# A state exchange layer on one core: one small-matmul stretch per batch, at the change of batch, in place of two

## The chip, the cores and the metric

The kernel runs on 1 core of one Trainium2 chip. The metric is the device time of one execution in microseconds (us). Before the change it was 646.53 us, the median of 3 runs (646.25 to 646.66).

## What is computed

The reference has two parts. The first, for each of 8 batches and 8 heads, exchanges 512 tokens `x` (512 x 64) with 32 states (32 x 64) by two softmaxes; the second sends the 4,352 rows that come out (8 batches x (512 tokens + 32 states), 512 wide) through two weight matrices.

```python
a  = softmax(x @ state.T / 8)        # over the 32 states
xread = a @ state                    # 512 x 64: what the tokens read
a2 = softmax(state @ x.T / 8)        # over the 512 tokens
sread = a2 @ x                       # 32 x 64: what the states read
x  = rows of [xread; sread], heads side by side   # 4352 x 512
h  = x @ w_in                        # 512 -> 2048
g  = where(h >= 1, h, where(h <= -1, 0, (h + 1)**2 / 4))
out = g @ w_out                      # 2048 -> 512
```

## The kernel before

**Order of the work.** The hidden width of 2048 is cut into 8 chunks of 256 (`NJ = 8`, index `j`). For a batch `b` and a chunk `j` the kernel makes `h` (`g1`, L488: two products of 6 matmuls each, L448 to L450), bends it to `g` on ACT and DVE (`relu`, `square`, `bound`, `high`, `low`), and adds `g` times a chunk of `w_out` to four accumulators of 128 tokens (`g2`, L502: 24 matmuls, L524 to L526). `g2` of a chunk is issued one step late, behind `g1` of the next chunk, so TensorE has work while ACT and DVE bend. Values are split into a high and a low part (`h` and `l` in the names), and each product is three matmuls: high x high, low x high, high x low. All of these big matmuls have a 128x128 tile of weights and 512 moving columns. A step of one chunk is 12 + 24 = 36 of them.

**No xread.** The kernel never forms `xread`. It multiplies the states of a batch with `w_in` first (`sw_product`, L371; tiles `sw_c`, named by the first chunk c that they hold), so that `h = a @ (state @ w_in)`. Such a product of one chunk is 16 small matmuls (L383, 64x32 of weights, 256 columns, 8 places of the array in turn). Two chunks together fill a pair of PSUM banks. ACT then copies the high part out (`sw_high`, L404, ACT instruction L623), and DVE subtracts to get the low part (`sw_low`, L408, L410); only then are the banks free. Eight chunks make four such pairs: chunks 1 and 2, 3 and 4, 5 and 6, and 7 with chunk 0 of the next batch.

**The attention of the next batch** runs beside this: `scores` (L217, 16 matmuls of 512 columns, tile `sc`), both softmaxes on DVE and ACT, and `shuffle`, 16 DMAs on SP's queue that turn the second softmax's weights (tile `e2`; `e` in the profile). `read2` (L326, L334: 64 small matmuls, 128x32 of weights and 64 columns, tile `sr`) forms `sread` from `e2` and the loaded `x` (tile `xn`, `load_xn`, L187). `scale2` (DVE, tile `rs`) divides by the sums. `keep2` (L346) turns the result with a TensorE transpose (tile `rt`, L348) and `keep` (L352) has ACT copy it into `srT`, which after the last batch goes through the two weight matrices as a last, ninth batch.

**PSUM.** There are eight banks: four accumulators (`ps_acc`, tag `acc`), two for `h` (`ps_h`), and one double tile (`ps_mm`) that scores, `sr` and `rt` share.

**What sets the order.** Batch 0 is emitted from an order written out by hand (`SEQ`), which the change does not touch. Batches 1 to 7 follow the program's loop (L875 on); within it, `later(place, b, j, ...)` hangs the attention's steps on a place of a step (`mid`: after `g1`; `end`: after `g2`). In a step with `j == 0` stands a stretch of small matmuls: the pairs 1, 3, the next scores, the pair 5. In the step with `j == 5`, between the two halves of `g2`, stands a second one: `read2` of the next batch and the pair 7. In batch 1 `read2` of its own states stands by itself behind `g1` of chunk 0. Each engine takes its instructions in order and waits with semaphores for others; SP's queue issues the DMAs in order.

Of the kernel before, what the change touches and what calls it, by code (L numbers as in the profile page):

```python
# [8 lines left out]
F32 = mybir.dt.float32  # L9
F32R = mybir.dt.float32r  # L10
# [94 lines left out]
def state_exchange_moe(  # L105
# [17 lines left out]
    nc = tc.nc  # L123
    B, P, NT, H, D = x.shape
    S = NT * P
    NS = 32
    DM = H * D
    NPR = H // 2
# [9 lines left out]
    small = ctx.enter_context(tc.tile_pool(name="small", bufs=1))  # L138
    const = ctx.enter_context(tc.tile_pool(name="const", bufs=1))
    work = ctx.enter_context(tc.tile_pool(name="work", bufs=2))  # L140
    ps = ctx.enter_context(tc.tile_pool(name="ps", bufs=2, space=PSUM))
    wop = ctx.enter_context(tc.tile_pool(name="wop", bufs=NJ))
    rawp = ctx.enter_context(tc.tile_pool(name="rawp", bufs=2))

    def ps_acc(name):
        return ps.tile([P, DM], F32, tag="acc", bufs=4, name=name)
# [4 lines left out]
    def ps_mm(name):  # L151
        return ps.tile([P, 2, 512], F32, tag="mm", bufs=1, name=name)
# [19 lines left out]
    srT = const.tile([P, NPR, B, NS], F32, name="srT")  # L172
# [5 lines left out]
    loaded = {}  # L178
# [8 lines left out]
    def load_xn(b):  # L187
        xn = work.tile([P, NT, H, D], F32, tag="xn", bufs=1, name=f"xn{b}")
        nc.sync.dma_start(out=xn, in_=x[b])
        return xn  # L190

    class Attention:
# [146 lines left out]
        def scale2(self):  # L339
# [3 lines left out]
                out=self.rs, in0=self.sr[:, :, :D], in1=self.r2[:, :, None].broadcast_to([P, 2, D]), op=ALU.mult  # L343
            )

        def keep2(self):  # L346
            self.rt = ps_mm(f"rt{self.b}")
            nc.tensor.transpose(  # L348
                out=self.rt[:, 0, :P], in_=self.rs.rearrange("p a d -> p (a d)"), identity=ident
            )  # L350
# [5 lines left out]

    def split_tiles(name, spare=False):
        if spare:  # L360
            both = rawp.tile([P, 2, 1024], F32R, tag="raw", name=f"{name}hl")
            return both[:, 0], both[:, 1]
        hi = work.tile([P, 1024], F32R, tag="wh", name=f"{name}h")
        lo = work.tile([P, 1024], F32R, tag="wl", name=f"{name}l")
        return hi, lo
# [2 lines left out]

    sw_of = {}

    def sw_product(items, apart=None, spare=False):  # L371

        b, c = items[0]
        if apart:
            banks = [apart(f"sw{b}_{c}_{hh}") for hh in range(2)]
        else:
            pt = ps_mm(f"sw{b}_{c}")
            banks = [pt[:, hh] for hh in range(2)]
        for i, (bi, ci) in enumerate(items):
            for pr in range(NPR):  # L380
                for hh in range(2):
                    rows = slice(hh * 64, hh * 64 + 64)
                    nc.tensor.matmul(  # L383
                        banks[hh][pr * NS:(pr + 1) * NS, i * CI:(i + 1) * CI],
                        lhsT=sb[rows, bi, pr], rhs=w32[ci][rows, pr], start=True, stop=True,
                    )
        w = len(items) * CI
        if b == 0 and c < NH:
            whole = work.tile([P, 1024], F32, tag="wh", name=f"sw{b}_{c}w").rearrange("p (q f) -> p q f", q=2)[:, :, :w]
            sw_of[b, c] = [(banks[q][:, :w], whole[:, q], None) for q in range(2)]  # L390
            chunk[b, c] = whole, None
            return
        wh, wl = (
            v[:, :2 * w].rearrange("p (q f) -> p q f", q=2) for v in split_tiles(f"sw{b}_{c}", spare)
        )
        if apart:
            sw_of[b, c] = [(banks[q][:, :w], wh[:, q], wl[:, q]) for q in range(2)]
        else:
            sw_of[b, c] = [(pt[:, :, :w], wh, wl)]
        for i, item in enumerate(items):  # L400
            cols = slice(i * CI, (i + 1) * CI)
            chunk[item] = wh[:, :, cols], wl[:, :, cols]

    def sw_high(b, c, engine="ACT"):  # L404
        for pt, wh, _ in sw_of[b, c]:
            copy(engine, wh, pt)

    def sw_low(b, c):  # L408
        for pt, wh, wl in sw_of[b, c]:
            nc.vector.tensor_tensor(out=wl, in0=pt, in1=wh.bitcast(F32), op=ALU.subtract)  # L410
# [91 lines left out]
    def g2(b, j, half=None):  # L502
        n = n_of[b]
        per = S // n
        nt = n // P
        if b not in acc:
            acc[b] = [ps_acc(f"acc{b}_{t}") for t in range(nt)]
        gh, gl = gs[b, j]
        last = j == NJ // per - 1
        pairs = [(i, t) for i in range(2 * per) for t in range(nt)]  # L510
        if last:
            pairs.sort(key=lambda p: p[1])
        if half is not None:
            pairs = pairs[half * len(pairs) // 2:][:len(pairs) // 2]
        for i, t in pairs:
            f = 2 * per * j + i
            oh, ol = wo[f // 2][:, 0, f % 2], wo[f // 2][:, 1, f % 2]
            c0 = (i % per) * n + t * P
            lh, ll = (v if v is None else v[:, i // per, c0:c0 + P] for v in (gh, gl))
            a = acc[b][t]  # L520
            if ll is None:
                nc.tensor.matmul(a, lhsT=lh, rhs=ol, start=f == 0, stop=False)
                continue
            nc.tensor.matmul(a, lhsT=lh, rhs=oh, start=f == 0, stop=False)  # L524
            nc.tensor.matmul(a, lhsT=lh, rhs=ol, start=False, stop=False)  # L525
            nc.tensor.matmul(a, lhsT=ll, rhs=oh, start=False, stop=f == NF - 1)  # L526
            if last and i == 2 * per - 1:
                store(b, t)
# [90 lines left out]
    def copy(engine, out, src):  # L619
        if engine == "DVE":  # L620
            nc.vector.tensor_copy(out, src)
        else:
            nc.scalar.copy(out=out, in_=src)  # L623
# [28 lines left out]
    atts = {}  # L652
# [153 lines left out]
    for word in GROUPS.split():  # L806
        c, n = word.split(".")
# [16 lines left out]
    def later(place, b, j, *items):  # L824
        for f, *a in items:
            background.setdefault((place, b, j), []).append((f, a))

    def issue(place, b, j):

        for f, a in background.get((place, b, j), ()):  # L830
            f(*a)

    def attention(b):

        def at(place, j, *names):
            for name in names:
                f, *q = name.split()
                later(place, b - 1, j, (lambda f=f, q=q: getattr(atts[b], f)(*map(int, q)),))

        at("end", 1, "turn 0", "turn 1", "top2 0")  # L840
        at("mid", 2, "exp2 0", "top2 1", "exp2 1", "top1 0", "top1 1", "turn_blocks 0")
        at("mid", 3, "turn_blocks 1", "shuffle")
        at("end", 3, "less1 0", "less1 1")
        at("end", 4, "exp1 0", "exp1 1", "sum1 0", "sum1 1", "inv1")
        at("mid", 5, "norm1 0", "norm1 1", "back 0", "back 1")
        at("mid", 6, "high1 0", "rest 0", "high1 1", "rest 1")
        at("end", 6, "keep2", "keep")

    def states_split():
        sh, sl = (work.tile([P, NPR, B * NS], F32R, tag=t, name=f"s{t}") for t in ("ath", "atl"))  # L850
# [2 lines left out]
        nc.vector.tensor_tensor(out=sl, in0=src, in1=sh.bitcast(F32), op=ALU.subtract)  # L853
        att_of[B] = (sh, sl)

    def load_later(b):
        loaded["xn", b] = load_xn(b)

    for name in ("read2", "scale2"):
        later("mid", 1, 0, (lambda name=name: getattr(atts[1], name)(),))  # L860
    later("mid", 1, 1, (load_later, 2))
    for name in ("keep2", "keep"):
        later("mid", 1, 3, (lambda name=name: getattr(atts[1], name)(),))
    for b in range(2, B):
        attention(b)
    for c in range(NG):
# [8 lines left out]
    with guard:  # L875
        plan.emit(warm, "sc.0.1", "g2.0.0.0")
        for i, (b, j) in enumerate(steps):
            if j == 0 and 1 < b < B - 1:
                load_later(b + 1)
            prior = steps[i - 1] if i else (0, NJ - 1)  # L880
            hid = g1(b, j, split=j or b == B)
            issue("mid", b, j)
            if j == 0 and b < B:
                g2(*prior, 0)
                hid.high()
                hid.low()
                g2(*prior, 1)
                sw_product([(b, 1), (b, 2)], ps_h)
                sw_product([(b, 3), (b, 4)], ps_acc)
                if b + 1 < B:  # L890
                    att_start(b + 1)
                sw_product([(b, 5), (b, 6)], ps_acc, True)
                for c in (1, 3, 5):
                    sw_high(b, c)
                    sw_low(b, c)
            elif j == 5 and b < B:
                g2(*prior, 0)
                if b + 1 < B:
                    atts[b + 1].read2()
                sw_product([(b, 7), (b + 1, 0)][:B - b], ps_h)  # L900
                sw_high(b, 7)
                sw_low(b, 7)
                if b + 1 < B:
                    atts[b + 1].scale2()
                g2(*prior, 1)
            else:
                g2(*prior)
            if j == 1 and b + 2 < B:
                loaded["xt", b + 2] = load_xt(b + 2)
            issue("end", b, j)  # L910
        g2(*steps[-1])


# [41 lines left out]
```

## Time and profile before

| | us |
|---|---|
| median of 3 runs | 646.53 |
| profiled execution | 646.69 |
| its span, first to last instruction | 644.9 |
| TensorE matmuls (PE) busy | 636.8 |
| TensorE weight loads (PEld) busy | 512.2 |
| ACT busy | 370.8 |
| DVE busy | 355.1 |
| mean granted TensorE clock | 1.000 |

Times are from the start of the span. PE is TensorE's matmuls, PEld its weight loads, which run beside them; DVE, ACT and SP are the vector, scalar and synchronization engines. L383 is line 383 of the kernel. A row of the timeline has the start, the length, the engine, the line, the operation, `out<-in`, the shapes and how many instructions in a row were merged; what the engine waited for stands in brackets behind. Matmuls are pipelined, so that the rows of a stream overlap: a big matmul shows 0.39 us, and the next starts 0.23 us later. What counts for TensorE is therefore the distance from start to start, not the busy time. A batch takes 71.6 us (its stretches in chunk 0 start at 99.77 and 171.53 us).

### The profile page before, as it was taken

Reading aid. Unit: us, or ns where it says so; the run is one execution under the profiler, and the core shown is the slowest. Engines: PE = TensorE matmul, PEld = TensorE weight load, DVE = VectorE, ACT = ScalarE, POOL = GpSimd, SP = SyncE. Lnnn points to the kernel's source line nnn. Section 1 sums busy time; section 2 is a strip of 40 time slices with the busy share of each in tenths; the row PEclk is TensorE's granted clock in tenths of the full one; section 3 lists DMA queues with packets and bytes.
Section 4 is the critical chain, followed back from the end, with each engine's and each line's share of the span. In section 5 each row is a group of like instructions: output and inputs, shape, how many; then the busy total and the mean of one; then the engine's idle time right before and its main releaser. Section 6 shows DMA issues by size and latency. Waiting matters only on the chain.

```text
span 644.9 us, 10366 instructions
## 1 busy us (share of the span) xinstructions
PE 636.8 (99%) x4358; PEld 512.2 (79%) x4358; DVE 355.1 (55%) x515; ACT 370.8 (57%) x542; POOL 0.8 (0%) x7
## 2 busy tenths in 40 slices
PE   8999999999999999999999999999999999999997
PEld 6667787878788787878788787878788778878896
DVE  5999965554465535664465535553465535335431
ACT  4999755555555555555755455545755455454641
POOL 0000000000000000000000000000000000000000
PEclk9999999999999999999999999999999999999999
DMA  8996115021201203030302212030102010000101
GB/s 354 415 373 233 41 21 197 0 52 48 106 26 28 71 16 116 6 93 2 131 1 33 67 41 90 14 87 1 66 1 33 1 67 2 1 0 1 66 1 33
DMA packets 41550, 47.33 MB, mean 73 GB/s; under 512 B 31776, under 2 KB 31904, under 8 KB 38432
## 3 DMA queue, kind: packets, MB, share of 16 engines
q1 hardware_dynamic: 41168, 46.35, 20.9%
q8 instruction: 34, 0.56, 0.4%
q10 hardware_dynamic: 336, 0.33, 0.2%
q14 instruction: 12, 0.10, 0.0%
HBM read 34.08 MB, written 8.91 MB: 67 GB/s over the span
## 4 chain that ended last, share of the span: by engine, by line
PE 94%; ACT 3%; DMA 1%; DVE 1%; issue 0%
PE acc L524 19%; PE acc L525 19%; PE acc L526 19%; PE h L448 10%; PE h L449 10%; PE h L450 10%; PE sw L383 4%; PE sc L217 1%; PE sr L334 1%; PE warmed L165 1%; DMA sb<-in_state_dram 1%; ACT u L465 1%; ACT raw_o L578 0%; ACT raw_i L578 0%; ACT raw_o L570 0%
## 5 line engine op out<-in xcount | busy, mean ns | idle before, releaser
L524 PE MATMUL acc<-wo,gh 128*128 128x512 f32 x544 | 213.2, 392 | 0.0
L525 PE MATMUL acc<-wo,gh 128*128 128x512 f32 x544 | 211.9, 390 | 0.1
L526 PE MATMUL acc<-wo,gl 128*128 128x512 f32 x544 | 211.8, 389 | 0.0
L472 DVE SCALAR_TENSOR_TENSOR u<-u,h 128x512 f32<-128x512 f32 x136 | 92.8, 687 | 180.2 <-ACT u L469 179.5
L465 ACT ACTIVATE u<-h,half 128x512 f32<-128x512 f32 x136 | 93.1, 690 | 159.0 <-PE h L450 156.7
L486 DVE TENSOR_TENSOR gl<-u,gh 128x1024 fp32r<-128x1024 f32 x68 | 83.3, 1225 | 75.8 <-ACT gh L623 75.7
L524 PEld LDWEIGHTS acc<-wo,gh 128*128 128x128 f32 x544 | 102.1, 188 | 26.3 <-issue 3.7
L526 PEld LDWEIGHTS acc<-wo,gl 128*128 128x128 f32 x544 | 102.1, 188 | 21.3
L525 PEld LDWEIGHTS acc<-wo,gh 128*128 128x128 f32 x544 | 102.2, 188 | 21.0 <-DVE wo L608 0.4
L623 ACT CAST gh<-u 128x1024 fp32r<-128x1024 f32 x68 | 71.5, 1052 | 40.8 <-DVE u L472 40.7
L469 ACT ACTIVATE u<-u 128x512 f32<-128x512 f32 (+1 forms) x128 | 84.5, 660 | 4.0
L383 PE MATMUL sw<-w,sb 64*32 64x256 f32 x1024 | 33.5, 380 | 0.0
L539 ACT COPY o<-acc 128x512 f32<-128x512 f32 x33 | 19.1, 586 | 16.6 <-PE acc L526 16.6
L383 PEld LDWEIGHTS sw<-w,sb 64*32 64x32 f32 x1024 | 17.9, 106 | 13.0 <-issue 7.6
L449 PE MATMUL h<-ath,sw_3l 128*128 128x512 f32 x64 | 25.0, 391 | 0.2 <-DVE sw_3l L410 0.2
L448 PE MATMUL h<-ath,sw_3h 128*128 128x512 f32 x64 | 25.0, 391 | 0.0
L450 PE MATMUL h<-atl,sw_3h 128*128 128x512 f32 x64 | 24.9, 390 | 0.0
L448 PE MATMUL h<-ath,sw_1h 128*128 128x512 f32 x60 | 24.3, 405 | 0.6 <-DVE u L472 0.6
L448 PE MATMUL h<-ath,sw_7h 128*128 128x512 f32 x60 | 23.9, 399 | 0.0
L450 PE MATMUL h<-atl,sw_1h 128*128 128x512 f32 x60 | 23.4, 390 | 0.0
L450 PE MATMUL h<-atl,sw_7h 128*128 128x512 f32 x60 | 23.4, 390 | 0.0
L449 PE MATMUL h<-ath,sw_1l 128*128 128x512 f32 x60 | 23.4, 390 | 0.0
(166 smaller groups left out, 711.9 us busy)
## 6 DMA issues: line engine op xcount, KB each, us to landing
xt<-in_xt_dram SPq DMA_DIRECT2D x16, 512.0 KB, 4.8
raw_i<-in_moe_w_in_dram SPq DMA_DIRECT2D x8, 1024.0 KB, 7.2
raw_o<-in_moe_w_out_dram SPq DMA_DIRECT2D x8, 1024.0 KB, 9.3
xn<-in_x_dram SPq DMA_DIRECT2D x8, 1024.0 KB, 5.6
out_dram<-o SPq DMA_DIRECT2D x32, 256.0 KB, 2.0
e<-eb SPq DMA_DIRECT2D x112, 32.0 KB, 2.0
sb<-in_state_dram SPq DMA_DIRECT2D x1, 448.0 KB, 11.6
out_dram<-o SPq DMA_DIRECT2D x4, 64.0 KB, 1.7
```

Source lines behind the costliest of these rows:

```text
L383: nc.tensor.matmul(banks[hh][pr * NS:(pr + 1) * NS, i * CI:(i + 1) * CI], lhsT=sb[rows, bi, pr], rhs=w32[ci][rows, pr], start=True, stop=True,
L448: nc.tensor.matmul(o, lhsT=wh[:, k, sl], rhs=ah[:, k], start=first, stop=False)
L449: nc.tensor.matmul(o, lhsT=wl[:, k, sl], rhs=ah[:, k], start=False, stop=False)
L450: nc.tensor.matmul(o, lhsT=wh[:, k, sl], rhs=al[:, k], start=False, stop=last)
L465: nc.scalar.activation(out=self.u[:, i], in_=self.hs[i], func=AF.Relu, scale=0.5, bias=half)
L469: nc.scalar.activation(out=u, in_=u, func=AF.Square)
L472: nc.vector.scalar_tensor_tensor(out=self.u[:, i], in0=self.u[:, i], scalar=1.0, in1=self.hs[i], op0=ALU.min, op1=ALU.max,)
L486: nc.vector.tensor_tensor(out=gl, in0=self.u, in1=gh.bitcast(F32), op=ALU.subtract)
L524: nc.tensor.matmul(a, lhsT=lh, rhs=oh, start=f == 0, stop=False)
L525: nc.tensor.matmul(a, lhsT=lh, rhs=ol, start=False, stop=False)
L526: nc.tensor.matmul(a, lhsT=ll, rhs=oh, start=False, stop=f == NF - 1)
L623: nc.scalar.copy(out=out, in_=src)
```

## The change

It puts all small matmuls of a batch into one stretch in the step with `j == 0`: `read2` of this batch's own states, the pairs 1, 3 and 5, the next scores, and the pair 7. The stretch in the step with `j == 5` goes, and so does batch 1's separate `read2`. What follows from it:

- The pairs 1, 5 and 7 go to accumulator banks and the pair 3 to the `h` banks. There are four accumulators, so the pair 7 takes those that the pair 1 filled.
- The split parts of the pair 5 are kept in the tile of `xn`, those of the pair 7 in one of `raw`'s (by `split_tiles`, L359, whose argument `spare` becomes `home`). `x` of the next batch is therefore loaded after the products of chunk 6, which are the last to read the pair 5, and is read in the next batch's chunk 0; before, it was loaded at the start of a batch and read in its chunk 5.
- For batches 1 to 7 `keep2` and `keep` are replaced by `place2`, in the step with `j == 1`: a DVE transpose of 32x32 blocks (tile `rt`) and 16 DMAs of 32x32 on SP's queue into `srT`.

```diff
+        def place2(self):
+            b = self.b
+            rt = small.tile([P, P], F32, tag="rt", name=f"rt{b}")
+            nc.vector.transpose(out=rt, in_=self.rs.rearrange("p a d -> p (a d)"))
+            for k in range(P // NS):
+                for pr in range(NPR):
+                    nc.sync.dma_start(
+                        out=srT[k * NS:(k + 1) * NS, pr, b], in_=rt[pr * NS:(pr + 1) * NS, k * NS:(k + 1) * NS]
+                    )
...
-        at("end", 6, "keep2", "keep")
...
-    for name in ("read2", "scale2"):
-        later("mid", 1, 0, (lambda name=name: getattr(atts[1], name)(),))
-    later("mid", 1, 1, (load_later, 2))
-    for name in ("keep2", "keep"):
-        later("mid", 1, 3, (lambda name=name: getattr(atts[1], name)(),))
+    for b in range(1, B):
+        later("mid", b, 1, (lambda b=b: atts[b].place2(),))
...
-            if j == 0 and 1 < b < B - 1:
-                load_later(b + 1)
...
-                sw_product([(b, 1), (b, 2)], ps_h)
-                sw_product([(b, 3), (b, 4)], ps_acc)
+                atts[b].read2()
+                sw_product([(b, 1), (b, 2)], ps_acc)
+                sw_product([(b, 3), (b, 4)], ps_h)
+                sw_product([(b, 5), (b, 6)], ps_acc, "xn")
+                atts[b].scale2()
                 if b + 1 < B:
                     att_start(b + 1)
-                sw_product([(b, 5), (b, 6)], ps_acc, True)
-                for c in (1, 3, 5):
+                sw_product([(b, 7), (b + 1, 0)][:B - b], ps_acc, "raw")
+                for c in (1, 3, 5, 7):
                     sw_high(b, c)
                     sw_low(b, c)
-            elif j == 5 and b < B:
-                g2(*prior, 0)
-                if b + 1 < B:
-                    atts[b + 1].read2()
-                sw_product([(b, 7), (b + 1, 0)][:B - b], ps_h)
-                sw_high(b, 7)
-                sw_low(b, 7)
-                if b + 1 < B:
-                    atts[b + 1].scale2()
-                g2(*prior, 1)
             else:
                 g2(*prior)
...
             issue("end", b, j)
+            if j == 6 and b + 1 < B:
+                loaded["xn", b + 1] = load_xn(b + 1)
```

How the instructions move shows best in batch 2. On TensorE before, its stretch in chunk 0 was this (of each pair of banks the first matmul into either bank, `sw_c_0` and `sw_c_1`; what it waits for stands behind it):

```order
L383 MATMUL sw_1_0_1604<-w_1_88,sb 32x256 [waits DVE_49]
L383 MATMUL sw_1_1_1605<-w_1_88,sb 32x256 [waits DVE_49]
...
L383 MATMUL sw_3_0_1624<-w_3_90,sb 32x256 [waits Activation_49]
L383 MATMUL sw_3_1_1625<-w_3_90,sb 32x256 [waits Activation_49]
...
L217 MATMUL sc_1646<-xt_1130,sb 32x512 [waits PE_49]
...
L383 MATMUL sw_5_0_1658<-w_5_92,sb 32x256 [waits Activation_49]
L383 MATMUL sw_5_1_1659<-w_5_92,sb 32x256 [waits Activation_49]
...
L448 MATMUL h_1_0_1690<-ath_1030,sw_1h 128x512 [waits DVE_49]
```

And in chunk 5 of the same batch, between the halves of `g2` (chunk 4's `gl` and `gh`), this one stood, with the read of batch 3 (`e_3`); the transpose of its result stands further on, ahead of chunk 7:

```order
L526 MATMUL acc_3_1717<-wo_611,gl_4_1902 128x512
L334 MATMUL sr_1977<-xn_1544,e_3_1747 32x64 [waits DMAHW4_49,DMAHW1_49,DMAHW0_49]
...
L383 MATMUL sw_7_0_2010<-w_7_94,sb 32x256 [waits DVE_49]
L383 MATMUL sw_7_1_2011<-w_7_94,sb 32x256 [waits DVE_49]
...
L524 MATMUL acc_0_1714<-wo_611,gh_4_1901 128x512
...
L348 MATMUL rt_2101<-ident,rs_2034 128x128 [waits DVE_49]
```

Now batch 2 has one stretch on TensorE, all of it in chunk 0:

```order
L334 MATMUL sr_1578<-xn_1469,e_2_1174 32x64 [waits DMAHW4_49,DMAHW0_49]
...
L393 MATMUL sw_1_0_1611<-w_1_88,sb 32x256 [waits Activation_49]
...
L393 MATMUL sw_3_0_1631<-w_3_90,sb 32x256 [waits DVE_49]
...
L393 MATMUL sw_5_0_1651<-w_5_92,sb 32x256 [waits Activation_49]
...
L217 MATMUL sc_1674<-xt_1169,sb 32x512 [waits DVE_49]
...
L393 MATMUL sw_7_0_1686<-w_7_94,sb 32x256 [waits DVE_49]
L393 MATMUL sw_7_1_1687<-w_7_94,sb 32x256 [waits DVE_49]
...
L458 MATMUL h_1_0_1722<-ath_1049,sw_1h 128x512 [waits DVE_49]
```

The read and the pair 7 have come into the stretch of chunk 0. The pair 7's wait for DVE is now one for `sw_low` of the pair 1, bank by bank, since it takes that pair's banks; that of `h_1_0` is for the pair 3. On DVE at the same place of the changed kernel the subtractions stand in this order, with `rs` (`scale2`) ahead of them:

```order
L496 TENSOR_TENSOR gl_0_1559<-u_0_1520,gh_0_1558 128x1024 [waits PE_49,Activation_49]
L342 TENSOR_TENSOR rs_1670<-sr_1578,r_2_1262 128x128 [waits PE_49]
L420 TENSOR_TENSOR sw_1l<-sw_1_0_1611,sw_1h 128x512 [waits Activation_49]
L420 TENSOR_TENSOR sw_1l<-sw_1_1_1612,sw_1h 128x512 [waits Activation_49]
L420 TENSOR_TENSOR sw_3l<-sw_3_0_1631,sw_3h 128x512 [waits Activation_49]
L420 TENSOR_TENSOR sw_3l<-sw_3_1_1632,sw_3h 128x512 [waits Activation_49]
```

Before, `rs` stood in chunk 5, behind the pair 7's subtractions; and `sw_1l` followed `gl_0` directly. The lines of the changed kernel are 10 further on from `read2`'s end (L383 is L393, L410 is L420, L448 is L458, L524 is L534).

More of the change, by code (lines that the diff above doesn't have):

```diff
@@ L355, in keep, with split_tiles @@
             )
-    def split_tiles(name, spare=False):
-        if spare:
-            both = rawp.tile([P, 2, 1024], F32R, tag="raw", name=f"{name}hl")
+    def split_tiles(name, home=None):
+        if home:
+            both = (rawp if home == "raw" else work).tile([P, 2, 1024], F32R, tag=home, bufs=2 if home == "raw" else 1, name=f"{name}hl")
             return both[:, 0], both[:, 1]
@@ L369, in state_exchange_moe, with sw_product @@
     sw_of = {}
-    def sw_product(items, apart=None, spare=False):
+    def sw_product(items, apart=None, home=None):
         b, c = items[0]
@@ L393, in sw_product @@
         wh, wl = (
-            v[:, :2 * w].rearrange("p (q f) -> p q f", q=2) for v in split_tiles(f"sw{b}_{c}", spare)
+            v[:, :2 * w].rearrange("p (q f) -> p q f", q=2) for v in split_tiles(f"sw{b}_{c}", home)
         )
@@ L854, in states_split @@
         att_of[B] = (sh, sl)
-    def load_later(b):
-        loaded["xn", b] = load_xn(b)
-    for name in ("read2", "scale2"):
-        later("mid", 1, 0, (lambda name=name: getattr(atts[1], name)(),))
-    later("mid", 1, 1, (load_later, 2))
-    for name in ("keep2", "keep"):
-        later("mid", 1, 3, (lambda name=name: getattr(atts[1], name)(),))
+    for b in range(1, B):
+        later("mid", b, 1, (lambda b=b: atts[b].place2(),))
     for b in range(2, B):
```

## The prediction

> **What bounds the kernel now.** I read the page first, then the list of TensorE's own waits, then TensorE's timeline around every place the change touches, and last the ACT, DVE and DMA rows there.
>
> ```profile
> PE 636.8 (99%) x4358; PEld 512.2 (79%) x4358; DVE 355.1 (55%) x515; ACT 370.8 (57%) x542; POOL 0.8 (0%) x7
> PE 94%; ACT 3%; DMA 1%; DVE 1%; issue 0%
> ```
>
> The first row is busy time, the second the chain that ended last: both are TensorE. Nothing is won on another engine; the time changes only by what TensorE does between its big matmuls (128x128 by 512 columns), whose pace two rows give (start, us; 15 matmuls lie between):
>
> ```profile
> 167.74 0.39 PE L526 MATMUL acc<-wo,gl 128*128 128x512 f32 x1
> ...
> 171.14 0.39 PE L526 MATMUL acc<-wo,gl 128*128 128x512 f32 x1
> 171.46 1.96 PE L383 MATMUL sw<-w,sb 64*32 64x256 f32 x64
> 173.21 1.06 PE L217 MATMUL sc<-xt,sb 64*32 64x512 f32 x16
> 174.07 1.07 PE L383 MATMUL sw<-w,sb 64*32 64x256 f32 x32
> 175.07 0.50 PE L448 MATMUL h<-ath,sw_1h 128*128 128x512 f32 x1
> 175.40 0.39 PE L449 MATMUL h<-ath,sw_1l 128*128 128x512 f32 x1
> 175.63 0.39 PE L450 MATMUL h<-atl,sw_1h 128*128 128x512 f32 x1
> ```
>
> The pace is 3.40/15 = 0.2267 us. So I price an interruption by one rule: the start of the third big matmul after it, less the start of the last one before it, less 3 x 0.2267 = 0.68. For the stretch above, which I call A (96 sw and 16 sc, batches 1 to 6): 175.63 - 171.14 - 0.68 = **3.81**.
>
> **The change part by part.** The other interruptions: the lone read of batch 1; the stretch in chunk 5 (B); its short form in batch 7 (B7); A of batch 7 (A7); a PE transpose (rt).
>
> ```profile
> 92.69 0.39 PE L450 MATMUL h<-atl,sw_7h 128*128 128x512 f32 x1
> 93.00 1.10 PE L334 MATMUL sr<-xn,e 128*32 128x64 f32 x64
> ...
> 94.61 0.39 PE L526 MATMUL acc<-wo,gl 128*128 128x512 f32 x1
> ...
> 122.26 0.39 PE L450 MATMUL h<-atl,sw_3h 128*128 128x512 f32 x1
> 122.49 0.27 PE L348 MATMUL rt<-ident,rs 128*128 128x128 f32 x1
> ...
> 123.06 0.39 PE L526 MATMUL acc<-wo,gl 128*128 128x512 f32 x1
> ...
> 213.06 0.39 PE L526 MATMUL acc<-wo,gl 128*128 128x512 f32 x1
> 213.38 1.10 PE L334 MATMUL sr<-xn,e 128*32 128x64 f32 x64
> 214.41 1.09 PE L383 MATMUL sw<-w,sb 64*32 64x256 f32 x32
> ...
> 216.00 0.40 PE L526 MATMUL acc<-wo,gl 128*128 128x512 f32 x1
> ...
> 218.29 0.44 PE L448 MATMUL h<-ath,sw_5hl 128*128 128x512 f32 x1
> 218.56 0.40 PE L449 MATMUL h<-ath,sw_5hl 128*128 128x512 f32 x1
> ...
> 529.21 0.39 PE L526 MATMUL acc<-wo,gl 128*128 128x512 f32 x1
> ...
> 532.85 0.39 PE L450 MATMUL h<-atl,sw_1h 128*128 128x512 f32 x1
> ...
> 570.26 0.39 PE L526 MATMUL acc<-wo,gl 128*128 128x512 f32 x1
> ...
> 571.73 0.40 PE L526 MATMUL acc<-wo,gl 128*128 128x512 f32 x1
> ```
>
> By the rule: lone read 1.24; rt 0.12; B 2.26; A7 (96 sw alone) 2.96; B7 (16 sw alone) 0.79. Behind B the first sw_5hl matmul starts 0.27 instead of 0.23 before the next: 0.05 late.
>
> From these the pieces: one sw matmul (2.96 - 0.79)/80 = 0.0271. What entering and leaving a stretch costs, whatever it holds: 0.79 - 16 x 0.0271 = **0.36**. The 16 sc: 3.81 - 2.96 = 0.85; with twice the columns of sw they would be 16 x 2 x 0.0271 = 0.87, so passing from sw to sc and back costs nothing. The 64 sr: 1.24 - 0.36 = 0.88. The step from sr to sw: 2.26 - 0.36 - 0.88 - 32 x 0.0271 = 0.15.
>
> What goes. Before, batches 1 to 7 pay 1.24 + 6 x 3.81 + 2.96 + 6 x 2.26 + 0.79 + 6 x 0.05 + 7 x 0.12 = 42.55. The matmuls themselves stay, save seven transposes; fifteen stretches become seven.
>
> What comes. A joined stretch of batches 1 to 6 is 0.36 + 0.88 + 0.15 + 128 x 0.0271 (3.47) + 0.85 = 5.71; that of batch 7, with no scores and 112 sw, 0.36 + 0.88 + 0.15 + 3.04 = 4.43. Sum 6 x 5.71 + 4.43 = 38.69. The saving is 42.55 - 38.69 = **3.86**: eight entries and exits 2.88, seven transposes 0.84, the late sw_5hl 0.30, less one step from sr to sw more. The bounds of the entry cost are 0.33 (what A leaves after 96 x 1.75/64 and the 0.86 between its sc and sw rows) and 0.39, so 0.25 either way.
>
> The Trainium skill (TensorEngine Tiling (Array Packing), Key Properties) says that changing the tiling mode drains the array, but not changing the tile. By that rule the price goes with changes of shape: 36 before (two in the lone read, A, A7 and B7, three in B), 21 after; at half of 0.36 each the saving would be 15 x 0.18 = 2.70 where mine is 2.88 - 0.15 = 2.73. The trace agrees: sw to sc, one shape, costs nothing.
>
> What may wait anew. The fourth pair of sw banks now takes the two accumulators that the first pair filled, so its first matmuls wait for DVE's two sw_1l subtractions, and everything behind on TensorE waits with them. The rows that time this in A (start and length; x2 is both halves), and a wait of the same kind in B:
>
> ```profile
> 172.64 1.07 ACT L623 CAST sw_1h<-sw 128x512 fp32r<-128x512 f32 x2 [0.49 <-PE sw L383]
> 173.26 1.29 DVE L410 TENSOR_TENSOR sw_1l<-sw,sw_1h 128x512 fp32r<-128x512 f32 x2 [1.62 <-ACT sw_1h L623]
> 174.47 1.28 DVE L410 TENSOR_TENSOR sw_3l<-sw,sw_3h 128x512 fp32r<-128x512 f32 x2
> 217.52 1.25 DVE L410 TENSOR_TENSOR sw_7l<-sw,sw_7h 128x512 fp32r<-128x512 f32 x2
> 218.23 0.19 PEld L448 LDWEIGHTS h<-ath,sw_5hl 128*128 128x128 f32 x1 [0.20 <-DVE sw_7l L410]
> L383 PEld LDWEIGHTS sw<-w,sb 64*32 64x32 f32 x1024 | 17.9, 106 | 13.0 <-issue 7.6 <-ACT u L465 0.4 <-ACT wo L623 0.4
> L342 DVE TENSOR_TENSOR rs<-sr,r 128x128 f32<-128x128 f32 x8 | 2.2, 274 | 0.0
> ```
>
> Count from the first sr. The first sw comes at 214.41 - 213.38 = 1.03. In A both sw_1l end 173.26 + 1.29 - 171.46 = 3.09 after the first sw, so now at 4.12; the wait in B ended about 0.03 after the first sw_7l (half of the 1.25 and a little), and a weight load is 0.11: the fourth pair can run from about 4.26. It is reached at 1.03 + 96 x 0.0271 + 0.85 = 4.48 in batches 1 to 6: covered by 0.22, so I take 0; the bound above is the whole wait of batch 7. There no scores lie between, it is reached at 3.63, and TensorE waits **0.63** once (from 0, if the trace's ACT work were earlier, to 0.9). Standing ahead of sw_1l on DVE is only rs, 0.27 us, ready when the reads end at 1.1, long before.
>
> Later reuse: the h banks of the second pair are free at 4.12 + 0.7 = 4.8 against 5.4 (in batch 7 about level); the third and fourth pairs' accumulators at 4.12 + 3 x 1.28 = 8.0 against 5.7 + 12 x 0.2267 = 8.4 for the first of g2, and later for the pair that is last. No wait.
>
> Off the path I cost at nothing:
>
> ```profile
> 199.55 10.39 SPq L322 DMA_DIRECT2D e<-eb x16
> xn<-in_x_dram SPq DMA_DIRECT2D x8, 1024.0 KB, 5.6
> L264 DVE STREAM_TRANSPOSE zt<-z 128x512 f32<-128x512 f32 x16 | 10.6, 691 | 0.0
> ```
>
> The DVE transpose of a quarter of 128x512 lies between 0.17 and 0.69; DVE is 45% idle, and ACT loses its copy. The 16 small DMAs hold SP for about 10.4 us as the like 16 of the shuffle do; behind them stand the xt load, wanted at the next stretch, some 50 us on, and the shuffle, whose result now also is wanted only there; the last batch's are read five chunks (5 x 36 x 0.2267 = 41 us) later. The x load moves behind the last use of chunk 6 and is wanted 96 big matmuls later, 21.8 us; it lands in 5.6. Behind it on SP, while it waits for chunk 6, stand only the batch's stores, which come later still. If that cover of 16 us were gone, every us beyond it would cost one in each of six batches.
>
> The profiled execution is 646.69 (span 644.9), the median of the runs 646.53. The sum is -3.86 + 0.63 = -3.23: 643.46 for the profiled one, **643.3** as a median. 0.2%, about what a measurement of this kernel can tell from no change, is 1.3 us.
>
> **The rivals.**
> *Emptying the banks decides (slower).* ACT and DVE need 1.28 us for a pair of banks that TensorE fills in 32 x 0.0271 = 0.87, and the joined stretch fills four pairs running. If sw_1l ended later by d, six batches would wait d - 0.22 and batch 7 0.63 + d; with one more pair (1.28) ahead of it that is 6 x 1.06 + 1.91 = 8.27, so 646.53 - 3.86 + 8.27 = 650.9. It decides from 7d - 0.69 = 3.86 + 1.3, d = 0.84. For it: the cover is only 0.22. Against: nothing but rs stands ahead of sw_1l, and the first pair is ready earlier than its banks are wanted. The Trainium skill (TensorEngine Tiling (Array Packing), PSUM Bottleneck) warns of just this, that tiling speeds TensorE but not the emptying of PSUM. Chance 0.03.
>
> *The cover fails by a little.* With d between 0.4 and 0.6, say because the reads end late, six waits of 0.2 to 0.4 leave 644.7 to 646.1. Chance 0.10, most of it still faster by over 0.2%.
>
> *Joining saves nothing.* If the 0.36 came with each change from one kind of matmul to another, the joined stretch would pay it inside, and only transposes, sw_5hl and the wait count: -0.84 - 0.30 + 0.63 = -0.5, 646.0. Against: sr to sw cost 0.15 in B, sw to sc nothing. Chance 0.05.
>
> *No wait in batch 7*, since ACT and DVE come to the first pair earlier: -3.86, 642.7. Chance 0.10.
>
> **How the numbers follow.** The forecast has the remaining 0.72, its own range 642.9 to 643.7. Below, the entry cost's upper bound without batch 7's wait gives 642.4; above I go to 645.2, where the six waits are 0.3. Outside lie the first rival, the third and the worse part of the second: about 0.12. Faster by over 0.2% (below 645.2): 0.72 + 0.10 + most of 0.10 = 0.90; within: 0.07; slower: 0.03.
>
> **What would show it.** In the changed kernel's timeline each batch has one run of sr, sw, sc, sw rows of about 5.7 us by my rule and none in chunk 5; no PE rt from batch 1 on; TensorE's list of waits has one of about 0.6 on sw_1l near 530 us and none elsewhere. Waits on sw_1l in every batch would mean the cover was too thin; a stretch well over 5.7 without a wait, that the entry cost isn't saved; a wait of sr for xn, that the load is late.

## The result, and the profile after

The changed kernel takes **642.8 us** (median of 4 runs, 642.02 to 642.88), beside 646.39 (645.51 to 646.66) for the kernel before on the same chip: a ratio of 0.9946, with a 95% interval of 0.9934 to 0.9958. That is 3.6 us less; 643.3 was forecast, 642.4 to 645.2 the range. The profiled execution took 642.83, its span is 641.0 (before 644.9), and the granted clock is 1.0 in both.

From the page of the changed kernel, the busy times, the chain that ended last, and two groups of DMA issues:

```profile
PE 631.9 (99%) x4351; PEld 513.5 (80%) x4351; DVE 356.6 (56%) x522; ACT 368.6 (57%) x535; POOL 0.8 (0%) x7
...
PE 94%; ACT 3%; DVE 2%; issue 1%; POOL 0%; POOLq 0%
...
xn<-in_x_dram SPq DMA_DIRECT2D x8, 1024.0 KB, 4.9
...
srT<-rt SPq DMA_DIRECT2D x112, 4.0 KB, 1.7
```

TensorE still sets the end; it has seven matmuls fewer (the transposes), DVE seven instructions more, ACT seven fewer, and SP's queue 112 small DMAs more.

The stretch of batch 5 on TensorE, from the last big matmul before it to the third behind it, and with it ACT's and DVE's work on the first pair (start, us):

```profile
381.81 0.39 PE L536 MATMUL acc<-wo,gl 128*128 128x512 f32 x1
382.13 1.10 PE L334 MATMUL sr<-xn,e 128*32 128x64 f32 x64
383.16 2.82 PE L393 MATMUL sw<-w,sb 64*32 64x256 f32 x96
385.78 1.06 PE L217 MATMUL sc<-xt,sb 64*32 64x512 f32 x16
386.63 1.07 PE L393 MATMUL sw<-w,sb 64*32 64x256 f32 x32
387.63 0.50 PE L458 MATMUL h<-ath,sw_1h 128*128 128x512 f32 x1
...
388.21 0.39 PE L460 MATMUL h<-atl,sw_1h 128*128 128x512 f32 x1
...
384.35 1.07 ACT L633 CAST sw_1h<-sw 128x512 fp32r<-128x512 f32 x2 [1.52 <-PE sw L393]
384.96 1.29 DVE L420 TENSOR_TENSOR sw_1l<-sw,sw_1h 128x512 fp32r<-128x512 f32 x2 [1.37 <-ACT sw_1h L633]
```

By the prediction's rule this stretch costs 388.21 - 381.81 - 0.68 = 5.72; on the unrounded times it is 5.715 in each of batches 1 to 5 (forecast 5.71). sw_1l ends 384.96 + 1.29 - 382.13 = 4.12 after the first sr, and the fourth pair starts at 386.63 - 382.13 = 4.50: both as worked out (4.12, 4.48), and the pair does not wait. Behind it the big matmuls run on without a break; the stretch in chunk 5 and the transposes on TensorE are gone.

Batches 6 and 7 differ. Batch 6 first; the two weight-load (PEld) rows show a gap of 0.19 us among the first scores, and nothing is named that ended it ("issue"):

```profile
456.57 0.32 PEld L217 LDWEIGHTS sc<-xt,sb 64*32 64x32 f32 x2
457.08 0.18 PEld L217 LDWEIGHTS sc<-xt,sb 64*32 64x32 f32 x14 [0.19 <-issue]
...
456.78 1.39 PE L217 MATMUL sc<-xt,sb 64*32 64x512 f32 x16
457.64 1.39 PE L393 MATMUL sw<-w,sb 64*32 64x256 f32 x32
```

The 16 scores take 1.39 instead of 1.06 us, and the stretch 6.035: 0.32 more that was not forecast. Batch 7:

```profile
524.15 0.39 PE L536 MATMUL acc<-wo,gl 128*128 128x512 f32 x1
...
525.50 3.81 PE L393 MATMUL sw<-w,sb 64*32 64x256 f32 x112
529.24 0.50 PE L458 MATMUL h<-ath,sw_1h 128*128 128x512 f32 x1
...
527.30 1.29 DVE L420 TENSOR_TENSOR sw_1l<-sw,sw_1h 128x512 fp32r<-128x512 f32 x2 [1.37 <-ACT sw_1h L633]
...
528.04 0.17 PEld L393 LDWEIGHTS sw<-w,sb 64*32 64x32 f32 x2 [0.21 <-DVE sw_1l L420]
528.64 0.18 PEld L393 LDWEIGHTS sw<-w,sb 64*32 64x32 f32 x14 [0.42 <-DVE sw_1l L420]
```

With no scores between, the fourth pair comes to the first pair's banks before the two sw_1l subtractions are done: the stretch takes 4.982 (its third big matmul behind starts at 529.81), that is 0.55 over the 4.43 without a wait (forecast 0.63). The wait is named on the weight loads alone (0.21 + 0.42); the merged matmul row hides it in its length, 3.81.

Where the 3.9 us of the two spans went: measured to the 20th big matmul behind each interruption instead of the third, all interruptions of batches 1 to 7 cost 43.22 us before and 39.69 after, so 3.53 is theirs. Another 0.34 lies ahead of batch 1's stretch, in code that the change does not touch: the last big matmul before it stands at 97.79, and in the kernel before, without its lone read, it would stand at 99.38 - 1.25 = 98.13. That part of the program differs between executions: the last big matmul ahead of batch 1's lone read stands at 92.69 in the kernel before and at 91.55 and 92.43 in the two kernels of experiments 1 and 2, which are the same up to there.

### The profile page after: what moved, and what is told of

Same layout as the page of the kernel before. It is cut to its first block, busy times and chain, and to the rows that moved or that the text cites. A ratio compares the mean times of both kernels' runs of the same rounds, so it can differ in the third digit from the quotient of the medians.

```text
span 641.0 us, 10497 instructions
## 1 busy us (share of the span) xinstructions
PE 631.9 (99%) x4351; PEld 513.5 (80%) x4351; DVE 356.6 (56%) x522; ACT 368.6 (57%) x535; POOL 0.8 (0%) x7
## 4 chain that ended last, share of the span: by engine, by line
PE 94%; ACT 3%; DVE 2%; issue 1%; POOL 0%; POOLq 0%
PE acc L534 19%; PE acc L535 19%; PE acc L536 19%; PE h L458 10%; PE h L459 10%; PE h L460 10%; PE sw L393 4%; PE sc L217 1%; PE sr L334 1%; ACT u L475 1%; PE warmed L165 1%; ACT raw_i L588 0%; DVE w L600 0%; ACT raw_o L588 0%; ACT gh L633 0%
## 5 line engine op out<-in xcount | busy, mean ns | idle before, releaser
L534 PE MATMUL acc<-wo,gh 128*128 128x512 f32 x544 | 212.3, 390 | 0.0
L534 PEld LDWEIGHTS acc<-wo,gh 128*128 128x128 f32 x544 | 102.1, 188 | 23.4 <-ACT raw_i L580 0.8
L393 PE MATMUL sw<-w,sb 64*32 64x256 f32 x1024 | 32.7, 379 | 0.5 <-DVE w L600 0.5
L393 PEld LDWEIGHTS sw<-w,sb 64*32 64x32 f32 x1024 | 20.0, 106 | 11.1 <-issue 3.8
L458 PE MATMUL h<-ath,sw_3h 128*128 128x512 f32 x64 | 25.0, 391 | 0.0
L458 PE MATMUL h<-ath,sw_1h 128*128 128x512 f32 x60 | 24.3, 405 | 0.6 <-DVE u L482 0.6
L458 PE MATMUL h<-ath,sw_5hl 128*128 128x512 f32 x56 | 21.8, 389 | 0.0
L459 PE MATMUL h<-ath,sw_5hl 128*128 128x512 f32 x56 | 21.8, 389 | 0.0
```

Of the source, the lines that this page charges most:

```text
L393: nc.tensor.matmul(banks[hh][pr * NS:(pr + 1) * NS, i * CI:(i + 1) * CI], lhsT=sb[rows, bi, pr], rhs=w32[ci][rows, pr], start=True, stop=True,
L458: nc.tensor.matmul(o, lhsT=wh[:, k, sl], rhs=ah[:, k], start=first, stop=False)
L459: nc.tensor.matmul(o, lhsT=wl[:, k, sl], rhs=ah[:, k], start=False, stop=False)
```

## The experiments

My theory is the prediction's: the saving is the entry and exit of stretches (0.36 us each time, less what a change of shape inside costs), plus the transposes; the only wait is batch 7's, on DVE's sw_1l, since the scores cover it elsewhere. Rivals: emptying the banks matters in every batch; joining itself saves nothing; SP's 112 new DMAs or the moved loads cost time. In each comparison the kernel before ran on the same chip: its median was 645.88 us beside the first seven of them, in both groups in which they ran, and its one time beside the last two 645.96.

**1. The placing by DVE and DMA alone**, in the kernel before (diff against before; `place2` is the change's own). It leaves both stretches as they were.

```diff
-        at("end", 6, "keep2", "keep")
+        at("end", 6, "place2")
...
-    for name in ("keep2", "keep"):
-        later("mid", 1, 3, (lambda name=name: getattr(atts[1], name)(),))
+    later("mid", 1, 3, (lambda: atts[1].place2(),))
```

Expected:

> The kernel before with one part of the change: the seven TensorE transposes of the states' read (and ACT's copies behind them) are replaced by the DVE transpose and 16 small DMAs; the stretches stay apart. Theory (each interruption of the big matmuls has a price of its own): seven times what a transpose costs by the trace of before, counted to the 20th big matmul after it (0.13 to 0.16), so 1.0 us faster than the kernel before, with no TensorE transpose rows from batch 1 on and every other interruption as it was. Rival (the joined stretch itself saves nothing, the gain comes from this route of the result): most of the 3.6 us of the change, 642.8 to 643.5. Second rival (the 16 DMAs per batch hold up the loads behind them): as slow as before or slower, with TensorE waiting for a DMA.

Measured: 655.33 us, a ratio of 1.0141 (1.0127 to 1.0155): slower by 9.5, where I had expected about 1 faster. The profiled execution, 654.07, is the shortest of the four, and one place in it shows the loss: batch 1's stretch in chunk 5, which costs 152.61 - 140.16 - 0.68 = 11.77 instead of 2.26 us. (The spans differ by 7.4: these 9.51, less 0.97 for the transposes, less 1.14 by which this execution stood earlier ahead of batch 1's first products, 98.24 for 99.38. What the other three executions lost beyond this is in no trace.) TensorE's rows there, and SP's queue ahead of them, in this kernel:

```profile
140.16 0.39 PE L536 MATMUL acc<-wo,gl 128*128 128x512 f32 x1
146.82 0.39 PE L334 MATMUL sr<-xn,e 128*32 128x64 f32 x2 [6.28 <-issue]
147.52 0.39 PE L334 MATMUL sr<-xn,e 128*32 128x64 f32 x2 [0.30 <-DMA e<-eb]
...
152.61 0.39 PE L536 MATMUL acc<-wo,gl 128*128 128x512 f32 x1
...
126.21 10.54 SPq L352 DMA_DIRECT2D srT<-rt  x16
136.87 10.45 SPq L322 DMA_DIRECT2D e<-eb  x16
```

and SP's queue in the kernel before:

```profile
127.78 10.76 SPq L322 DMA_DIRECT2D e<-eb  x16
```

The 16 small DMAs of the placing take 10.54 us of SP's time, and I had put them ahead of the shuffle's 16, on which the read waits: the shuffle begins 136.87 - 127.78 = 9.1 us later, and 10.4 later beside TensorE's own work, which stands 1.27 earlier here (140.16 for 141.43). The read goes on as the shuffle's parts land. The 6.28 us of "issue" I take for the same wait, since the rows behind it name the shuffle's DMA; the profile itself names no releaser there. A part of the 9.51 comes behind the wait: from 144.69 to 151.52 us the granted clock is 0.5 in this trace (1.0 there in the kernel before), and the last 58 sr and the 32 sw take 1.84 and 1.44 us from start to start, beside about 0.93 and 1.03 elsewhere, so 1.3 more.

What follows: 16 DMAs on SP are not free, they have to be hidden. In the change they stand in chunk 1, and they are through before the shuffle begins:

```profile
111.33 10.37 SPq L352 DMA_DIRECT2D srT<-rt  x16
...
128.08 11.36 SPq L322 DMA_DIRECT2D e<-eb  x16
```

The shuffle is not held up by them: it begins 128.08 - 97.79 = 30.3 us after the last big matmul ahead of batch 1's stretch, before 127.78 - 99.38 = 28.4, and the stretch itself has become 1.9 longer. Besides, its result is now wanted only in the next batch's chunk 0, from 169 us on. The rival on SP's queue is true as a mechanism and has its price, 9.5 us for one batch, where the DMAs stand ahead of a shuffle that is wanted soon.

**2. The placing alone, one step later** (as 1, but `later("mid", 1, 4, ...)`, behind the shuffle).

> The kernel before with the DVE transpose and the 16 DMAs in place of TensorE's transposes, as in the first run of this kind, but in batch 1 one chunk later, so that its 16 DMAs stand behind the 16 of the shuffle on SP's queue and not ahead of them. Theory of the queue (in that run the read of batch 2 waited 9.5 us for a shuffle that stood 10.5 us behind those DMAs): the wait goes, every read shows 2.26 by the rule of the third big matmul, and the time is 0.7 to 1.0 us below the kernel before, which is what seven TensorE transposes cost by its trace. Rival (the small DMAs or the DVE transpose themselves hold something up): the read of batch 2 still waits, several us slower than before.

Measured: 644.98 us, ratio 0.9987 (0.9978 to 0.9996), 0.9 us faster than before. All reads cost 2.26 again:

```profile
141.04 0.39 PE L536 MATMUL acc<-wo,gl 128*128 128x512 f32 x1
141.36 1.10 PE L334 MATMUL sr<-xn,e 128*32 128x64 f32 x64
...
143.98 0.40 PE L536 MATMUL acc<-wo,gl 128*128 128x512 f32 x1
...
127.53 10.79 SPq L322 DMA_DIRECT2D e<-eb  x16
138.43 21.65 SPq L352 DMA_DIRECT2D srT<-rt  x24
```

143.98 - 141.04 - 0.68 = 2.26. The same DMAs stand behind the shuffle and cost nothing (the last row merges batch 1's 16 with the first 8 of batch 2). Seven transposes are worth 0.9 by the medians, 0.97 by the sum to the 20th matmul (43.22 to 42.24): 0.14 each, where the prediction's rule saw 0.12.

**3. The read by itself again** (diff against the changed kernel).

```diff
                 hid.low()
-                g2(*prior, 1)
                 atts[b].read2()
+                g2(*prior, 1)
```

> The changed kernel with the 64 matmuls of the read taken out of the joined stretch and put between the two halves of the last chunk's accumulation, 2.7 us earlier: one stretch more per batch, nothing else. Theory: each of the seven batches pays one more entry and exit, 0.36 and a slow restart of 0.01 to 0.1, less the step from the read to the products that goes (0.15): 7 x 0.22 to 0.30 = 1.5 to 2.1 us slower than the changed kernel, so 1.5 to 2.1 faster than the kernel before; the lone read should show 1.25 by the rule of the third big matmul, as it did in batch 1 of before. Rival (price by change of kind of matmul, not by stretch): the read apart changes kind as often, so no difference from the changed kernel, within 0.3.

Measured: 644.12 us, ratio 0.9967 (0.9955 to 0.998), the change's being 0.9946 (0.9934 to 0.9958) and, in the run further down, 0.9943. Batch 5 in this kernel, a lone read and 12 big matmuls on, the rest:

```profile
380.09 0.39 PE L536 MATMUL acc<-wo,gl 128*128 128x512 f32 x1
380.41 1.10 PE L334 MATMUL sr<-xn,e 128*32 128x64 f32 x64
...
382.01 0.39 PE L536 MATMUL acc<-wo,gl 128*128 128x512 f32 x1
...
384.06 0.39 PE L536 MATMUL acc<-wo,gl 128*128 128x512 f32 x1
...
389.42 0.40 PE L460 MATMUL h<-atl,sw_1h 128*128 128x512 f32 x1
```

382.01 - 380.09 - 0.68 = 1.24 and 389.42 - 384.06 - 0.68 = 4.68: together 5.92, where joined they cost 5.72. Seven batches at 0.20 (0.24, counted to the 12th matmul) are 1.4 to 1.7 us, less a pause in batch 6 that this kernel doesn't have (below); the difference of the ratios is 1.4 to 1.6. The intervals of the ratios touch, so the traces carry this more than the times. So joining saves, and as much as an entry and exit (0.36) less the step from sr to sw (0.15). The rival "joining saves nothing" is out. The Trainium skill's rule (TensorEngine Tiling (Array Packing), Key Properties), that a change of tiling mode drains the array, gives nearly the same here, 0.18 for the measured 0.20: the split kernel has one change of shape more per batch, at half of 0.36 each.

**4. The scores last**, so that the fourth pair comes right behind the third in every batch.

```diff
+                sw_product([(b, 7), (b + 1, 0)][:B - b], ps_acc, "raw")
                 if b + 1 < B:
                     att_start(b + 1)
-                sw_product([(b, 7), (b + 1, 0)][:B - b], ps_acc, "raw")
```

> The changed kernel with the next scores moved behind the last pair of products, so that in batches 1 to 6, as in batch 7, no scores lie between the third pair and the fourth, which takes the first pair's banks. Theory of the bank wait: the cover of 0.85 goes and each of these six batches waits 0.5 to 0.6 on the subtraction of the first pair, as batch 7 does: 3.0 to 3.6 us slower than the changed kernel, about as slow as before. Rival (the wait of batch 7 has another cause that is batch 7's own): no difference, within 0.3.

Measured: 645.5 us, ratio 0.9994 (0.9985 to 1.0003): nearly all of the gain is gone. The six stretches cost 6.26 to 6.27 instead of 5.715, batch 7 as before 4.99. The stretch of batch 5, from the last big matmul before it to the third behind it (390.86 - 383.92 - 0.68 = 6.26), and two rows of this kernel's list of waits (us in total, times, longest):

```profile
383.92 0.39 PE L536 MATMUL acc<-wo,gl 128*128 128x512 f32 x1
...
390.86 0.39 PE L460 MATMUL h<-atl,sw_1h 128*128 128x512 f32 x1
...
PEld h L458 <- DVE sw_5hl L420: 5.0, 6, 0.8
PEld sw L393 <- DVE sw_1l L420: 4.4, 14, 0.4
```

and of the changed kernel's:

```profile
PEld sw L393 <- DVE sw_1l L420: 0.8, 3, 0.4
```

Six times 0.55 is 3.3. The waits on sw_1l account for it, 0.63 on the weight loads of each batch. The row on sw_5hl I read as no wait of the matmuls: it is the load of h behind the scores, such a load idles 0.41 in batch 5 of the change too, where no matmul waits, and the six stretches lose no more than batch 7, which has no scores. The 0.85 us of scores between third and fourth pair is the whole cover, and it is enough. This is the first rival of the prediction, made to happen: the Trainium skill (TensorEngine Tiling (Array Packing), PSUM Bottleneck) warns that emptying PSUM may not keep up with a tiled TensorE, and the runs agree as soon as four pairs are filled without a break.

**5. Batch 7's fourth pair in the double tile** that scores and read share, so that it does not wait for sw_1l.

```diff
-                sw_product([(b, 7), (b + 1, 0)][:B - b], ps_acc, "raw")
+                sw_product([(b, 7), (b + 1, 0)][:B - b], ps_acc if b + 1 < B else None, "raw")
```

> The changed kernel with one difference: in batch 7, which has no next scores, the last chunk's product goes to the double tile that the scores would have used, and not to the first pair's banks. Theory: the wait of batch 7 goes, its stretch falls from 4.98 to about 4.45 by the rule of the third big matmul, so 0.5 us faster than the changed kernel (642.3). Rival (something else is late there too, the h banks of the second pair): the wait stays in the row behind and nothing is gained.

Measured: 642.69 us, ratio 0.9948 (0.9934 to 0.9961): no gain, and batch 7's stretch still costs 4.994. The expectation missed, and the rival named there was right. The matmuls of this kernel show where the wait went:

```profile
525.29 3.25 PE L393 MATMUL sw<-w,sb 64*32 64x256 f32 x112
529.04 0.50 PE L458 MATMUL h<-ath,sw_1h 128*128 128x512 f32 x1 [0.49 <-DVE sw_3l L420]
```

The 112 sums now run through in 3.25, but the next h wants the banks of the second pair, and DVE is no further with sw_3l. The prediction had this second limit as "about level" in batch 7; removing the first shows that it was.

**6. All of batch 7's banks dealt again**: the first pair into the h banks, the second into accumulators, the fourth into the double tile.

```diff
-                sw_product([(b, 1), (b, 2)], ps_acc)
-                sw_product([(b, 3), (b, 4)], ps_h)
+                sw_product([(b, 1), (b, 2)], ps_acc if b + 1 < B else ps_h)
+                sw_product([(b, 3), (b, 4)], ps_h if b + 1 < B else ps_acc)
...
-                sw_product([(b, 7), (b + 1, 0)][:B - b], ps_acc, "raw")
+                sw_product([(b, 7), (b + 1, 0)][:B - b], ps_acc if b + 1 < B else None, "raw")
```

> The changed kernel with other banks in batch 7 alone: the first pair of products goes to the h banks, which the next product wants first, the second and third to the four accumulators, and the last chunk to the double tile that has no scores there. Theory: the run before showed that with the last chunk in the double tile the wait only moved to the h banks, whose subtraction (of the second pair) was as late; now the h banks hold the pair that is emptied first, so batch 7's stretch falls from 4.98 to about 4.45 by the rule of the third big matmul, 0.5 us faster than the changed kernel, with no wait of TensorE near 525 us. Rival (the stretch of batch 7 takes 4.98 for what it holds, not for a wait): 4.98 again.

Measured: 641.64 us (641.44 to 642.67), ratio 0.9937 (0.9925 to 0.995). Beside it ran **7, the change once more, unedited**:

> The changed kernel once more, on the same chip as the two beside it. Theory: 3.5 us below the kernel before, its stretches 5.71 to 5.72 in batches 1 to 5 and 4.98 in batch 7; the extra 0.3 of batch 6's stretch in the first trace is either there again (then it belongs to the program) or not (then to that execution).

Measured: 642.06 us (641.89 to 642.68), ratio 0.9943 (0.993 to 0.9955). Batch 7 in the kernel with the banks dealt again:

```profile
524.85 1.10 PE L334 MATMUL sr<-xn,e 128*32 128x64 f32 x64
525.88 3.25 PE L393 MATMUL sw<-w,sb 64*32 64x256 f32 x112
529.06 0.50 PE L458 MATMUL h<-ath,sw_1h 128*128 128x512 f32 x1
```

The sums take 3.25 and h follows at once: the stretch costs 4.422, the prediction's 4.43 without a wait, against 4.975 in run 7. So the wait is gone in the trace, 0.55 us of it. In the times this version beats the kernel before and lies 0.42 below the change, but the two intervals overlap; the gain over the change is shown by the trace alone. The two profiled executions have the same span, 640.9: there the gain is hidden by batch 6's pause, which here was 0.45 and in run 7 only 0.10, and by 0.22 more ahead of batch 1's stretch (98.04 for 97.82).

**8 and 9. The pause of batch 6.** The change and its near variants show it: 0.32 in the change, 0.10 in run 7 with the same program, 0.19 in experiment 5, 0.45 in 6. Experiments 3 and 4 don't show it. Is it the scores of that batch, or a place in the program? Two kernels are that of experiment 6 with more warm-up at the head, `WARM = 7` made `WARM = 20` and `WARM = 52`, so that all that follows is shifted in TensorE's program. One step of that number is two matmuls; the shift was 26 and 90 matmuls, not the 13 and 45 of the expectations.

> This is the version with batch 7's pairs in other banks, with 13 more warm-up matmuls (26 more instructions on TensorE's queue with their weight loads) at the head, ahead of the first input's arrival, so that every later instruction stands 26 places further in the program. The question is the pause in batch 6's stretch (0.45 us in that version, 0.32 in the change, at the first two weight loads of the scores, ended by nothing that the profile shows). Theory 'place in the program': the pause sits where the instruction stream is cut, and so 13 matmuls earlier in the work: in the pair before the scores, with the scores' matmuls of batch 6 at their 1.06 us, or it goes from that stretch and shows in another. Rival 'the scores themselves' (batch 6's rows or banks): the pause stays at the scores' first two weight loads and the 16 matmuls take 1.3 to 1.5 us again. The span stays within 0.6 us of 640.9 by both.

> As the run with 13 more warm-up matmuls, but 45 more (90 instructions), which put about 1 to 6 us on the head. Theory 'place in the program': batch 6's pause lies 45 matmuls earlier in the work than in the unshifted version, in the pair of sums before the last, or is gone from that stretch. Rival 'the scores themselves': it stays at the scores' first two weight loads, 0.1 to 0.5 us, and the 16 matmuls take 1.2 to 1.5 us. The stretches of batches 1 to 5 stay at 5.7 us by both.

Measured, one run each: 645.87 and 652.8 us (before: 645.96), spans 644.1 and 651.0. The span moved by more than I had expected: batch 1's stretch starts 3.1 and 9.9 us later, 0.12 and 0.11 for each added matmul. The first input's arrival hides next to nothing: it held up the first scores for 0.26 us in experiment 6, and they start at 9.04 and 15.87 instead of 5.07. Batch 6 and batch 7 with the smaller shift:

```profile
460.16 1.06 PE L217 MATMUL sc<-xt,sb 64*32 64x512 f32 x16
461.02 1.07 PE L393 MATMUL sw<-w,sb 64*32 64x256 f32 x32
...
528.55 2.31 PEld L393 LDWEIGHTS sw<-w,sb 64*32 64x32 f32 x86
531.27 0.60 PEld L393 LDWEIGHTS sw<-w,sb 64*32 64x32 f32 x26 [0.42 <-issue]
```

and batch 4 with the larger one:

```profile
325.03 0.36 PEld L217 LDWEIGHTS sc<-xt,sb 64*32 64x32 f32 x12
325.62 0.14 PEld L217 LDWEIGHTS sc<-xt,sb 64*32 64x32 f32 x4 [0.24 <-issue]
```

With the smaller shift batch 6 has no pause (5.715) and batch 7 has one of 0.55, inside its sums, where no scores are. With the larger one batches 3 and 4 pause 0.31 and 0.36, and batches 6 and 7 do not (5.715 and 4.422). The expectation that batches 1 to 5 stay at 5.7 failed there. So it does not belong to the scores, their rows or their banks; it moves with the place in the program (the shift moves all times too, so the place is the likely cause, not the only thing that was changed). The DMA records bear on why: in each of these seven cases (0.32, 0.10, 0.19, 0.45; 0.55; 0.31, 0.36) a transfer on the instruction queue began 1.4 to 1.8 us after the last big matmul, and TensorE's last matmul before the pause began 2.0 to 2.6 us after it. For experiment 6, the DMA queues in the window from 454 to 456 us (packets, MB, share of 16 engines):

```profile
q8 instruction: 1, 0.02, 4.6%
```

Where it began at another time, no joined stretch paused. But one at 1.75 (batch 5 of the larger shift) brought no pause where one at 1.76 (batch 6 of the change) did, and in experiment 3 two at 1.55 and 1.63 of the shorter stretch brought none. In experiment 4 two more (1.58 and 1.74) added nothing to stretches that wait for their banks at that moment anyhow. That TensorE ran out of instructions there is likely, since it takes a matmul every 27 ns in a stretch and one every 227 outside, but it is inferred from the times alone. What sets when such a transfer begins stays open.

## Why the prediction was right

- **What a joined stretch costs: right.** 5.71 was forecast, 5.715 measured in five batches. The price of entering and leaving (0.36), the step from sr to sw (0.15) and the free step to sc and back held in a combination that no trace before had shown; splitting the read off again (experiment 3) gave back the 0.20 that these prices make.
- **What goes: right in kind, too small by 0.67.** The rule stopped at the third big matmul. After an interruption the stream runs slowly for longer: counted to the 20th matmul, the second stretch cost 2.35 with the late sw_5hl where I took 2.31, a transpose 0.13 to 0.16 where I took 0.12, A 3.84 where I took 3.81. Before paid 43.22, not 42.55. What comes suffers much less, since seven interruptions are left of 22.
- **The wait in batches 1 to 6: right.** The cover held: sw_1l was done at 4.12 as forecast, the fourth pair came at 4.50 for 4.48, and experiment 4 shows what it covers, 0.55 a batch. The first rival's mechanism is real; only the order of scores and fourth pair keeps it out.
- **The wait in batch 7: right, 0.55 for 0.63**, and with the second limit that was called level right behind it (experiments 5 and 6).
- **The transposes, SP's DMAs and the moved load: right.** 0.9 for 0.84 by experiment 2. The 16 DMAs are hidden in the change; experiment 1 shows the price if the cover were gone. No wait on TensorE's list names xn.
- **Not seen: batch 6's pause**, 0.32 in the profiled execution. Between the 3.23 forecast and the 3.53 measured in the stretches 0.67 more goes, and 0.37 more comes: the pause, and 0.05 that is slow restarts less the shorter wait. With the 0.34 ahead of batch 1 that is the 0.63 between 643.46, the forecast for the profiled execution, and its 642.83. That the median, 642.8, lies 0.5 below the forecast and just outside the forecast's own range of 642.9 to 643.7 is the sum of these misses, and that it is no more is partly luck: the unforeseen pause takes back half of the 0.67, and the 0.34 belongs to no term of the prediction.

## What to carry to other kernels

Price an interruption of a stream of matmuls from start to start, and count to the tenth or twentieth matmul behind it, not the third; then split it into a fixed entry, the matmuls and the changes of shape, and the price of another grouping can be added up. When work is joined, look for what used to stand between: here 0.85 us of scores is all that keeps TensorE from waiting for the banks, and whether they stand ahead of the fourth pair or behind it decides over some 3 of the 3.6 us. Small DMAs off the path hold their queue for 0.6 to 0.7 us each, so look at who stands behind them, not only at when they land.

## What the runs showed of the hardware that was not expected

- Small matmuls can run into a pause of 0.1 to 0.55 us that nothing in the profile releases, that moves with the place in the program, and that in seven of seven cases followed the start of a transfer on the instruction queue by 2.0 to 2.6 us (such a transfer does not always bring one); one program showed 0.32 and 0.10 in two executions.
- A wait on DVE can show on the weight loads (PEld) alone and disappears in a merged matmul row, whose length alone gives it away (3.81 for 3.25). And a wait named on a weight load need not be one of the matmuls: the load of h idles 0.41 "for DVE" in batch 5 of the change, where the matmuls run on.
- The 16 DMAs of the placing (4 KB each) hold SP for 10.0 to 11.8 us, the shuffle's 16 (32 KB each) for 10.4 to 11.5: their count matters, hardly their bytes.
- In the one trace with a long wait of TensorE in mid-stream (experiment 1, no matmul starts between 140.16 and 146.82) the granted clock was 0.5 from 144.69 to 151.52 us, so the wait went on costing after it had ended.
- An isolated 128x128 transpose in the stream costs 0.12 at the third big matmul behind it and up to 0.16 at the twentieth.
